# A mixture-of-experts tail in which the second expert's units, too, are taken from counts that are not final yet

## The chip, the cores and the metric

The kernel runs on one core of a Trainium2 chip. Its time is the device time in microseconds, 736.81 us as the median of three runs (733.63 to 736.97). The core's engines appear in the profile as PE (TensorE matmul), PEld (TensorE weight load), DVE (VectorE), ACT (ScalarE), POOL (GpSimd) and SP (SyncE, which here only issues DMAs and loads registers).

## The reference, cut to what matters

Three layers follow one another on 2304 tokens of 512 features: attention in a window of 64, a dense MLP with a squared ReLU, and a mixture of eight experts in which every token goes to the one expert with the largest gate logit.

```python
attn_out = _attn_ref(q, k, v)                       # (4, 8, 576, 64), window 64, softmax
x = attn_out.transpose(0, 2, 1, 3).reshape(2304, 512)
h = np.maximum(x @ w_in, 0.0)                       # moe_w_in  (512, 2048)
x = h * h @ w_out                                   # moe_w_out (2048, 512)
logits = x @ w_gate + modality_bias[modality_id]    # 8 experts
e_idx = np.argmax(logits, axis=1)
gate_w = softmax(logits)[arange, e_idx]
for e in range(8):
    mask = e_idx == e
    h = np.maximum(x[mask] @ w1[e], 0.0)            # w1 (8, 512, 1024)
    out[mask] = gate_w[mask, None] * (h @ w2[e])    # w2 (8, 1024, 512)
```

The gate's bias depends on one of two modalities of a token and is large beside the rest of the logit. On the inputs as they are drawn (seed 0) all 2304 tokens go to two experts: 1136 to expert 7, which is also the expert of token 0, and 1168 to expert 4. Of the first 14 blocks of 128 tokens (1792 tokens) 893 go to expert 7 and 899 to expert 4.

## The kernel before, in words

All matrix products are done as three products of 32-bit parts (`PASSES`): each weight chunk of 128x512 is loaded by SP into a staging tile `st`, ACT writes its high part into `w` (`split_hi`, L429) and DVE the low part (`split_lo`, L432). The ring of weights has 8 slots; an expert needs 4 of them (two halves of w1, two of w2), that is 16 chunks.

The dense MLP runs over groups of 256 or 512 tokens. After each block of 128 tokens its gate is computed in small steps by DVE (`gate_steps`): one-hot expert, position of each token in its expert's list (`pi`), and the running counts `noff`. POOL then scatters the token numbers into the table `tbl` in DRAM (L585) and writes the token rows `x2` into `xs` (L588). The table has a stretch of EST slots for each expert.

The mixture of experts works in **units** of 256 tokens (two halves of 128) of one expert. For a unit, `gather` reads the token numbers from the table (`ix`), fetches the rows of `xs` by an indirect DMA on POOL (L765), `transp` transposes them on PE (L307, tile `ps_x`) into `xh` and `xl`, and `moe2_job` runs L1 (L477, tile `l`, 24 matmuls for each of four steps) and L2 (L536, tile `acc`, 12 matmuls for a step). At a unit's end the two halves are scaled and scattered to the output by POOL (L806). L1 of the next step is emitted ahead of L2 of the present one, so a unit's last L2 stands behind the next unit's first L1. A unit takes about 22 us.

Which tokens belong to which unit is known only when all 18 blocks are gated; `list_steps` then works out a list on DVE. So that PE has work until then, the first three units (0, 1, 2) are **guessed**: their expert is that of token 0 (`e0i`), and their 768 tokens are the first 768 of that expert among the first 14 blocks (GUESS_TT = 14). Units 0 and 1 run while the last four blocks are gated and the list is worked out. Unit 2 runs after it. Behind it come, in the order of `seq`, listed unit 3, a wide unit `w` of 384 tokens that takes an odd rest, and listed units 4 to 7; each loads the 16 chunks of its own expert anew (`add_expert`). With the draw above `w` holds 368 tokens of expert 7, and units 3 to 7 hold the 1168 tokens of expert 4. Further units exist under a condition (`extra`) and are skipped when the list is short enough.

The order on each engine is that of emission by the functions below, made by a scheduler that may move an instruction ahead of one that it does not depend on. `u_work` decides at which step of a unit the next one's rows are gathered, how many chunks are split, and when the list's expert and base of the one after are loaded into registers (`prep`, SP's L1018 and L1019). When the gate's buffers are given up (`gate_ctx.close()`), their memory becomes the pools `wide` and `stage3`; a DMA into `stage3` waits until the last DMA out of the old `x2` tiles has landed.

Of the kernel before, what the change touches and what calls it, by code (L numbers as in the profile page):

```python
# [1 line left out]
KN = {'at1': ((0, 3, 4, 5), (3, 6, 7, 8), (6, 9, 10, 11), (9, 12, 13, 14)),  # L2
# [4 lines left out]

# [6 lines left out]
FP32 = mybir.dt.float32  # L14
F32R = mybir.dt.float32r
BF16 = mybir.dt.bfloat16
I32 = mybir.dt.int32
# [37 lines left out]
def kernel(  # L55
# [21 lines left out]
    LIST = 16  # L77
# [1 line left out]
    U_STATIC = 8  # L79
    GUESS_TT = 14  # L80
    GUESS = 3
    U_MAX = GUESS + LIST
    SCALE = 0.125
    ROW = DM + 1
    EST = NT + 256
# [33 lines left out]
    e0f = const.tile([128, 1], FP32, name="e0f")  # L119
    e0i = const.tile([128, 1], I32, name="e0i")  # L120
    b0i = const.tile([128, 1], I32, name="b0i")
    st0 = const.tile([128, E], FP32, name="st0")
    ewi = const.tile([128, LIST], I32, name="ewi")
    bsi = const.tile([128, LIST], I32, name="bsi")
# [420 lines left out]
    def gate_steps(tt, x2, per):  # L545
        lg = small.tile([128, E], FP32, tag="lg", name="lg")
        nl = small.tile([128, E], FP32, tag="nl", name="nl")
        sc = small.tile([128, E], FP32, tag="sc", name="sc")
        oh = small.tile([128, E], BF16, tag="oh", name="oh")
        nm = small.tile([128, 1], FP32, tag="gm", name="gm")  # L550
        mx = small.tile([128, 1], FP32, tag="gx", name="gx")
        sm = small.tile([128, 1], FP32, tag="gs", name="gs")
        pf = small.tile([128, 1], FP32, tag="pf", name="pf")
        pi = small.tile([128, 1], U32, tag="pi", name="pi")
        for e in range(E):
            nc.vector.tensor_tensor_reduce(out=gp["junk"], in0=x2[:, 0:DM], in1=gp["wgb"][:, e, :], scale=1.0, scalar=0.0,  # L556
                                           op0=ALU.mult, op1=ALU.add, accum_out=lg[:, e:e + 1])
            if e % per == per - 1:
                yield
        nc.vector.tensor_tensor_reduce(out=nl, in0=lg, in1=bsel[:, tt, :], scale=-1.0, scalar=3.0e38,  # L560
                                       op0=ALU.add, op1=ALU.min, accum_out=nm)
        nc.scalar.activation(out=lg, in_=nl, func=ACTF.Exp, scale=-1.0, bias=nm, accum_out=sm)
        nc.vector.scalar_tensor_tensor(out=sc, in0=nl, scalar=nm, in1=rev8, op0=ALU.is_equal, op1=ALU.mult)
        nc.vector.tensor_reduce(out=mx, in_=sc, axis=AX.X, op=ALU.max)
        nc.vector.tensor_scalar(out=oh, in0=sc, scalar1=mx, scalar2=None, op0=ALU.is_equal)
        nc.vector.tensor_scalar(out=sm, in0=sm, scalar1=1e-9, scalar2=None, op0=ALU.add)
        nc.vector.reciprocal(out=x2[:, DM:DM + 1], in_=sm)
        for _ in range(KN['y']):
            yield True
        ps = bank([128, 3, E], "ps_r")  # L570
        nc.tensor.matmul(out=ps[:, 0, :], lhsT=upper, rhs=oh, start=True, stop=True)
        nc.tensor.matmul(out=ps[:, 1, :], lhsT=ones, rhs=oh, start=True, stop=True)
        if tt == 0:
            nc.tensor.matmul(out=ps[:, 2, :], lhsT=row0, rhs=oh, start=True, stop=True)
        assert state["n"] == tt
        state["n"] += 1
        off = state["off"]
        noff = small.tile([128, E], FP32, tag="off", name="off")
        nc.vector.tensor_tensor(out=sc, in0=ps[:, 0, :], in1=off, op=ALU.add)
        nc.vector.tensor_tensor_reduce(out=lg, in0=sc, in1=oh, scale=1.0, scalar=0.0,  # L580
                                       op0=ALU.mult, op1=ALU.add, accum_out=pf)
        nc.vector.tensor_copy(pi, pf)  # L582
        nc.vector.tensor_tensor(out=noff, in0=ps[:, 1, :], in1=off, op=ALU.add)
        state["off"] = noff
        nc.gpsimd.indirect_dma_start(  # L585
            out=tbl[:, :], out_offset=bass.IndirectOffsetOnAxis(ap=pi[:, 0:1], axis=0),
            in_=tid[:, tt:tt + 1], in_offset=None, bounds_check=NSLOT - 1, oob_is_err=False)
        nc.gpsimd.dma_start(out=xs[128 * tt:128 * (tt + 1), :], in_=x2)  # L588
        if tt == 0:
            nc.vector.tensor_copy(e0oh, ps[:, 2, :])  # L590
            nc.vector.tensor_tensor_reduce(out=nl, in0=e0oh, in1=iota8, scale=1.0, scalar=0.0,
                                           op0=ALU.mult, op1=ALU.add, accum_out=e0f)
            nc.vector.tensor_copy(e0i, e0f)
            nc.vector.tensor_scalar(out=e0f, in0=e0f, scalar1=float(EST), scalar2=None, op0=ALU.mult)
            nc.vector.tensor_copy(b0i, e0f)
        if tt == GUESS_TT - 1:
            t8 = small.tile([128, E], FP32, tag="t8", name="t8", bufs=1)
            nc.vector.tensor_tensor(out=t8, in0=noff, in1=base8, op=ALU.subtract)
            nc.vector.tensor_tensor(out=st0, in0=t8, in1=e0oh, op=ALU.mult)
            nc.vector.tensor_scalar(out=st0, in0=st0, scalar1=256.0 * GUESS, scalar2=None, op0=ALU.min)  # L600
        yield

    def list_steps():
# [145 lines left out]
    rows = {}  # L749
    late = {}  # L750

    def gather(u, base, n):
        assert state["n"] >= (GUESS_TT if u in range(GUESS) else NTT)
        nh = 3 if u == "w" else 2
        sfx = "w" if u == "w" else ""
        pool = gp["wide"] if u == "w" else late["row"]
        ix = late["row"].tile([128, nh], I32, tag="ix" + sfx, name="ix" + sfx, bufs=1 if u == "w" else 3)
        eng = nc.gpsimd if u in range(GUESS) else nc.sync
        eng.dma_start(out=ix, in_=tbl[bass.ds(base, 128 * nh), :].rearrange("(h p) o -> p (h o)", p=128))
        r = []  # L760
        for hf in range(nh):
            t = pool.tile([128, ROW], FP32, tag="row", name="row")
            nc.gpsimd.memset(t, 1.0)
            ia = ix[:, hf:hf + 1].bitcast(U32)
            nc.gpsimd.indirect_dma_start(  # L765
                out=t[:, :], out_offset=None, in_=xs[0:n, :],
                in_offset=bass.IndirectOffsetOnAxis(ap=ia, axis=0),
                bounds_check=n - 1, oob_is_err=False)
            r.append((t, ia))
        rows[u] = r  # L770
# [15 lines left out]
    def moe2_job(u):  # L786
        job = Job()
        job.n, job.square = 4, False
        if u == "w":
            job.n, job.fb, job.cols = 8, 1, WIDE  # L790
        job.wkey = 0 if u in range(GUESS) else u
        job.x = [x[:, :, 0:job.cols] for x in xt_t.pop(("u", u))]
        r = rows.pop(u)

# [178 lines left out]
    def last_work(s):  # L973
        if s == 0:
            dma_chunks(KN["nb"])
        if s >= KN['lsp']:
            split_steps(1)
        slot(2 if s < KN['lsp'] else 1)
        for u, at in enumerate(KN['lg']):
            if s == at:  # L980
                gather(u, bv0 + 256 * u, 128 * GUESS_TT)

    def last_pieces(s):
        if s == KN['lt']:
            transp(0)

    run(moe1_job(GROUPS[-1][0], 2), last_work, last_pieces)

    def u0_work(s):
        if s == KN['ul']:  # L990
# [8 lines left out]

    def u1_work(s):  # L1000
        slot(KN['u1'])

    run(moe2_job(0), u0_work, u_next(0))
    run(moe2_job(1), u1_work, u_next(1))
# [8 lines left out]
    def prep(u):  # L1013
        if u == "w":
            ew, bw = wei[0:1, 0:1], wbi[0:1, 0:1]
        else:
            ew, bw = ewi[0:1, u - GUESS:u - GUESS + 1], bsi[0:1, u - GUESS:u - GUESS + 1]
        ev = nc.sync.value_load(ew, min_val=0, max_val=E - 1)  # L1018
        evs[u] = nc.sync.value_load(bw, min_val=0, max_val=NSLOT - WIDE)  # L1019
        add_expert(u, ev)  # L1020

    seq = list(range(GUESS - 1, U_STATIC))
    seq.insert(KN["seqw"], "w")
    prep(seq[1])
    dma_chunks(KN["nb2"])

    def u_work(i, wide):
        nxt = seq[i + 1] if i + 1 < len(seq) else None

        def f(s):  # L1030
            if nxt is None or (wide and s % 2):
                return
            s = s // 2 if wide else s
            if s == KN['g']:
                gather(nxt, evs[nxt], NT)
            split_steps(KN['sp' if i else 'sp0'][s])
            if s == KN['prep'] and i + 2 < len(seq):
                prep(seq[i + 2])
        return f

    def u_pieces(i, wide):
# [11 lines left out]
    def extra(u):  # L1053
        if u >= U_MAX:
            return
        with tc.If(tot > u - GUESS):
            prep(u)
            gather(u, evs[u], NT)
            dma_chunks(KN["nb2"])
            split_steps(17)  # L1060
            transp(u)
            run(moe2_job(u), nothing, nothing)
            flush()
            extra(u + 1)
# [53 lines left out]
```

## Time and profile before

| | |
|---|---|
| median of 3 runs | 736.81 us (733.63 to 736.97) |
| the profiled execution | 735.87 us, of which the span is 734.2 us |
| mean granted TensorE clock | 0.985 |
| PE busy | 699.3 us (95%) |
| DVE, ACT busy | 448.4 us (61%), 356.8 us (49%) |
| POOL busy | 89.7 us (12%) |
| moved by DMA | 84.49 MB, 115 GB/s over the span |
| weight chunks split in the mixture of experts | 112 (ACT 63.8 us, DVE 72.1 us) |

How to read it: the time beside the span is 1.67 us of start and end. A share of busy time is a mean over stages; the mixture of experts begins at about 497 us of the span, and what happens there is read from views of that stretch. Times in rows are microseconds from the span's start; the number in square brackets is the idle time of that engine just before, with what ended it.

### The profile page before, as it was taken

To read this page: it belongs to the slowest core of one execution; us is meant where nothing else is said; L and a number is where in the kernel's file an instruction comes from. 1 tells how busy PE (TensorE), PEld (TensorE's weight loads), DVE (VectorE), ACT (ScalarE), POOL (GpSimd) and SP (SyncE) were. 2 spreads that over 40 slices of the span, in tenths; PEclk is the share of its full clock that TensorE was granted. 3 is DMA by queue.
4 is the path that set the end of the run, shared out by engine and by line. 5 is a ranking of instruction groups with operands and counts; after the bars stand their busy time and mean duration, and the time that the engine had idled before them with its cause. 6 is when DMAs were issued, how large, how long until landed. Compare 5 with 4: busy or idle time off the path is not lost. (4 is left out here: it accounts for less than half of the span.)

```text
span 734.2 us, 13351 instructions
## 1 busy us (share of the span) xinstructions
PE 699.3 (95%) x4777; PEld 599.7 (82%) x4777; DVE 448.4 (61%) x1394; ACT 356.8 (49%) x841; POOL 89.7 (12%) x126
## 2 busy tenths in 40 slices
PE   6499999999999999999999999999996999999995
PEld 5398789888888888778888888888895988999994
DVE  3988997598665534685633794219846664477511
ACT  4867777565255345535434465433115553555410
POOL 3000000010000000010001110221313311112211
PEclk9899999999999999999999999999998999999998
DMA  7876651435222013204300168130248864577400
GB/s 209 278 235 203 197 178 37 169 108 115 42 69 80 30 50 66 66 30 79 80 31 5 68 60 127 30 87 16 53 60 264 270 201 160 173 239 248 144 29 21
DMA packets 62412, 84.49 MB, mean 115 GB/s; under 512 B 26016, under 2 KB 35248, under 8 KB 62208
## 3 DMA queue, kind: packets, MB, share of 16 engines
q1 hardware_dynamic: 57136, 69.26, 35.2%
q0 software_dynamic: 5200, 14.29, 6.1%
q8 instruction: 39, 0.64, 0.4%
q14 instruction: 37, 0.30, 0.1%
HBM read 74.23 MB, written 9.82 MB: 114 GB/s over the span
## 5 line engine op out<-in xcount | busy, mean ns | idle before, releaser
L477 PE MATMUL l<-xh,w 128*128 128x256 f32 (+2 forms) x1344 | 320.3, 320 | 0.0
L536 PE MATMUL acc<-w,hh 128*128 128x512 f32 x880 | 277.2, 395 | 0.0
L477 PEld LDWEIGHTS l<-xh,w 128*128 128x128 f32 x1344 | 228.5, 191 | 19.4 <-issue 1.5
L477 PE MATMUL l<-xl,w 128*128 128x256 f32 (+2 forms) x672 | 213.8, 318 | 0.0
L536 PEld LDWEIGHTS acc<-w,hh 128*128 128x128 f32 x880 | 160.0, 188 | 30.8 <-ACT hh L495 0.4
L536 PE MATMUL acc<-w,hl 128*128 128x512 f32 x440 | 172.3, 392 | 2.4 <-DVE hl L503 2.2
L477 PEld LDWEIGHTS l<-xl,w 128*128 128x128 f32 x672 | 128.4, 191 | 9.4 <-DVE xl L784 0.4
L489 ACT ACTIVATE hr<-l 128x512 f32<-128x512 f32 x72 | 42.7, 593 | 127.8 <-PE l L477 110.8
L503 DVE TENSOR_TENSOR hl<-hr,hh 128x512 fp32r<-128x512 f32 x72 | 49.7, 690 | 90.1 <-ACT hr L500 89.7
L536 PEld LDWEIGHTS acc<-w,hl 128*128 128x128 f32 x440 | 82.6, 188 | 22.1 <-DVE hl L503 3.1
L556 DVE CUSTOM_DVE_ANT_0 junk<-x,wgb 128x512 bf16<-128x512 f32 x144 | 98.9, 687 | 2.4 <-ACT x L742 0.2
L432 DVE TENSOR_TENSOR w<-st,w 128x512 fp32r<-128x512 f32 x112 | 72.1, 685 | 16.6 <-ACT w L429 16.4
L429 ACT CAST w<-st 128x512 fp32r<-128x512 f32 x112 | 63.8, 618 | 15.4 <-DMA st<-in_moe_w_dram 15.0
L274 ACT ACTIVATE p<-p,nm 128x128 f32<-128x128 f32 x144 | 55.9, 390 | 22.5 <-DVE nm L265 22.4
L516 ACT ACTIVATE hh<-l 128x512 fp32r<-128x512 f32 (+1 forms) x40 | 23.0, 574 | 82.5 <-PE l L477 82.5
L517 DVE SCALAR_TENSOR_TENSOR hl<-l,hh 128x512 fp32r<-128x512 f32 (+1 forms) x40 | 26.5, 662 | 58.8 <-ACT hh L516 58.5
L588 POOL DMA_DIRECT2D xs<-x x18 | 10.3, 574 | 304.4 <-DVE lg L556 145.9
L495 ACT ACTIVATE hh<-hr 128x512 fp32r<-128x512 f32 x72 | 45.5, 632 | 3.5 <-PE acc L536 1.5
L500 ACT ACTIVATE hr<-hr 128x512 f32<-128x512 f32 x72 | 45.5, 632 | 1.9
L585 POOL DMA_INDIRECT tbl<-tid,pi x18 | 19.4, 1079 | 159.4 <-DVE pi L582 123.1
L307 PE MATMUL ps_t<-ident,p 128*128 128x128 f32 x144 | 23.7, 291 | 12.9 <-DVE p L299 6.4
L307 PEld LDWEIGHTS ps_t<-ident,p 128*128 128x128 f32 x144 | 18.0, 149 | 17.0 <-ACT p L274 12.7
(146 smaller groups left out, 570.3 us busy)
## 6 DMA issues: line engine op xcount, KB each, us to landing
st<-in_moe_w_dram SPq DMA_DIRECT2D x112, 256.0 KB, 4.0
vt<-in_v_dram SPq DMA_DIRECT2D x35, 256.0 KB, 3.9
st<-in_moe_w_out_dram SPq DMA_DIRECT2D x16, 512.0 KB, 3.7
kt<-in_k_dram SPq DMA_DIRECT2D x17, 384.0 KB, 4.2
st<-in_moe_w_in_dram SPq DMA_DIRECT2D x12, 512.0 KB, 4.7
xs<-x POOLq DMA_DIRECT2D x18, 256.5 KB, 3.7
qt<-in_q_dram SPq DMA_DIRECT2D x36, 128.0 KB, 4.7
st<-in_moe_w_in_dram SPq DMA_DIRECT2D x8, 256.0 KB, 5.0
```

Source lines behind the costliest of these rows:

```text
L274: nc.scalar.activation(out=p[:, pr, :], in_=p[:, pr, :], func=ACTF.Exp, scale=-1.0, bias=nm[:, pr:pr + 1], accum_out=sm[:, pr:pr + 1])
L307: nc.tensor.transpose(out, in_, ident)
L429: nc.scalar.copy(out=part(where, 0, src), in_=src)
L432: eng.tensor_tensor(out=part(where, 1, src), in0=src, in1=part(where, 0, src).bitcast(FP32), op=ALU.subtract)
L477: nc.tensor.matmul(out=ps[:, job.cols * j:job.cols * (j + 1)], lhsT=wt[:, a, kk, f0:f0 + 128], rhs=job.x[b][:, kk, :], start=(kk == 0 and ...
L489: nc.scalar.activation(out=e["r"], in_=ps, func=ACTF.Relu)
L495: nc.scalar.activation(out=e["hh"], in_=e["r"], func=ACTF.Square)
L500: nc.scalar.activation(out=e["r"], in_=e["r"], func=ACTF.Square)
L503: nc.vector.tensor_tensor(out=hl, in0=e["r"], in1=e["hh"].bitcast(FP32), op=ALU.subtract)
L517: nc.vector.scalar_tensor_tensor(out=hl, in0=ps, scalar=0.0, in1=hh.bitcast(FP32), op0=ALU.max, op1=ALU.subtract)
L536: nc.tensor.matmul(out=job.acc[th], lhsT=h[a][:, c0:c0 + 128], rhs=wt[:, b, c, :], start=(mp == 0 and j == 0 and n == 0), stop=(mp == last ...
L556: nc.vector.tensor_tensor_reduce(out=gp["junk"], in0=x2[:, 0:DM], in1=gp["wgb"][:, e, :], scale=1.0, scalar=0.0, op0=ALU.mult, op1=ALU.add ...
```

## The change

A second expert is guessed as well. When block 13 is gated, DVE takes from the counts the expert with the most tokens other than the first guess (`e1oh`, `e1i`, `b1i`). Units 0 to 2 are guessed for the first expert, units 3 to 5 for the second; each three share one load of weights (`wkey`). The listed units are only 6 and 7, and the wide unit stands between unit 5 and unit 6. The list starts from counts without the 2 x 768 guessed tokens (`st0`). The table's entries of three units are read by one DMA on POOL (`guess_ix`). From unit 2 on rows are gathered two units ahead instead of one, and the chunks are split by a table of their own for each unit (`spl`). With the draw above `w` holds the same 368 tokens, and units 6 and 7 the remaining 400 of expert 4; the number of units is the same.

```diff
-      ... 'prep': 2, 'g': 1, 'seqw': 2}
+      ... 'prep': 2, 'g': 1, 'seqw': 4, 'gl': 4, 'spl': ([2, 2, 2, 2, 2, 2, 2, 3], [0] * 8, [1] * 8, [1] * 8, [2, 2, 2, 2, 2, 2, 2, 3], [2, 2, 2, 2, 2, 2, 2, 3], [0] * 8)}
...
-    U_MAX = GUESS + LIST
+    NGU = 2 * GUESS
+    U_MAX = NGU + LIST
...
         if tt == GUESS_TT - 1:
...
+            V.tensor_tensor(out=t8, in0=noff, in1=base8, op=ALU.subtract)
+            V.scalar_tensor_tensor(out=e1oh, in0=e0oh, scalar=-4096.0, in1=t8, op0=ALU.mult, op1=ALU.add)
+            V.scalar_tensor_tensor(out=e1oh, in0=e1oh, scalar=8.0, in1=rev8, op0=ALU.mult, op1=ALU.add)
+            V.tensor_reduce(out=e1f, in_=e1oh, axis=AX.X, op=ALU.max)
+            V.tensor_scalar(out=e1oh, in0=e1oh, scalar1=e1f, scalar2=None, op0=ALU.is_equal)
+            V.tensor_tensor_reduce(out=nl, in0=e1oh, in1=iota8, scale=1.0, scalar=0.0,
+                                   op0=ALU.mult, op1=ALU.add, accum_out=e1f)
+            V.tensor_copy(e1i, e1f)
+            V.tensor_scalar(out=e1f, in0=e1f, scalar1=float(EST), scalar2=None, op0=ALU.mult)
+            V.tensor_copy(b1i, e1f)
+            V.tensor_tensor(out=e1oh, in0=e0oh, in1=e1oh, op=ALU.add)
+            V.tensor_tensor(out=st0, in0=t8, in1=e1oh, op=ALU.mult)
+            V.tensor_scalar(out=st0, in0=st0, scalar1=256.0 * GUESS, scalar2=None, op0=ALU.min)
...
+    def guess_ix(u, base):
+        t = late["row"].tile([128, 2 * GUESS], I32, tag="ixg", name="ixg", bufs=2)
+        nc.gpsimd.dma_start(out=t, in_=tbl[bass.ds(base, 256 * GUESS), :].rearrange("(h p) o -> p (h o)", p=128))
+        for k in range(GUESS):
+            ixs[u + k] = t[:, 2 * k:2 * k + 2]
...
-        job.wkey = 0 if u in range(GUESS) else u
+        job.wkey = u // GUESS * GUESS if u in range(NGU) else u
...
-                gather(u, bv0 + 256 * u, 128 * GUESS_TT)
+                if u == 0:
+                    guess_ix(0, bv0)
+                    bv1 = nc.gpsimd.value_load(b1i[0:1, 0:1], min_val=0, max_val=(E - 1) * EST)
+                    guess_ix(GUESS, bv1)
+                gather(u, None, 128 * GUESS_TT)
...
+    ev1 = nc.sync.value_load(e1i[0:1, 0:1], min_val=0, max_val=E - 1)
...
     def u1_work(s):
         slot(KN['u1'])
+        if s == 0:
+            add_expert(GUESS, ev1)
+            dma_chunks(KN["nb"])
+        if s == KN['g']:
+            gather(3, None, 128 * GUESS_TT)
...
-    prep(seq[1])
-    dma_chunks(KN["nb2"])
+
+    PREP = {1: "w", 3: NGU, 4: NGU + 1}
...
-            if s == KN['g']:
-                gather(nxt, evs[nxt], NT)
-            split_steps(KN['sp' if i else 'sp0'][s])
-            if s == KN['prep'] and i + 2 < len(seq):
-                prep(seq[i + 2])
+            if s == KN['g' if i < 3 else 'gl'] and i + 2 < len(seq):
+                u = seq[i + 2]
+                gather(u, evs.get(u), 128 * GUESS_TT if u in range(NGU) else NT)
+            split_steps(KN['spl'][i][s])
+            if s == KN['prep'] and i in PREP:
+                prep(PREP[i])
+            if s > KN['prep'] and i == 1:
+                dma_chunks(1)
...
-        with tc.If(tot > u - GUESS):
+        with tc.If(tot > u - NGU):
```

Up to the end of unit 1, PE's and ACT's instructions stand as before. What moves is shown at three places.

**POOL, from the end of unit 0 on.** `x2_...` are unit 0's two output halves (DMA to `out_dram`) and the last block's rows (DMA to `xs`); `row` are gathered rows, here those of unit 3. Before:

```order
L806 DMA out_dram<-x_5752,ix 2304x512
L763 MEMSET row 128x513 x2
L806 DMA out_dram<-x_5763,ix 2304x512
L585 DMA tbl<-tid,pi 25600x1
L588 DMA xs<-x_5461 128x513
L585 DMA tbl<-tid,pi 25600x1
L763 MEMSET row 128x513 x3
L765 DMA row<-xs,ix 128x513 x2
L806 DMA out_dram<-o,ix 2304x512
```

Now:

```order
L832 DMA out_dram<-x_5789,ixg 2304x512
L789 MEMSET row 128x513
L791 DMA row<-xs,ixg 128x513
L789 MEMSET row 128x513
L832 DMA out_dram<-x_5800,ixg 2304x512
L791 DMA row<-xs,ixg 128x513
L588 DMA tbl<-tid,pi 25600x1
L591 DMA xs<-x_5490 128x513
L588 DMA tbl<-tid,pi 25600x1
L789 MEMSET row 128x513 x3
L832 DMA out_dram<-o,ixg 2304x512
```

Unit 3's two gathers stand ahead of the last two table scatters and the last write of `xs`, where they stood behind them.

**SP, around the list's registers.** `wei`, `wbi`, `toti`, `ewi`, `bsi` are the list's results, `st_...` staging tiles, `ix_...` the table entries of unit 3. Before:

```order
L1018 TENSOR_LOAD ewi_104
L396 DMA st_6016<-in_moe2_w1_dram 128x512
L1019 TENSOR_LOAD bsi_105
L396 DMA st_6018<-in_moe2_w1_dram 128x512
...
L396 DMA st_6026<-in_moe2_w2_dram 128x512
L759 REGISTER_ALU
L759 DMA ix_6079<-tbl_88 128x2x1
```

Now:

```order
L399 DMA st_5777<-in_moe2_w1_dram 128x512
L1055 TENSOR_LOAD wei_109
L1056 TENSOR_LOAD wbi_109
L1089 TENSOR_LOAD toti_108
L1055 TENSOR_LOAD ewi_106
L399 DMA st_6072<-in_moe2_w2_dram 128x512
L399 DMA st_6076<-in_moe2_w2_dram 128x512
...
L399 DMA st_6154<-in_moe2_w1_dram 128x512
```

The second expert's first four chunks (the last of them `st_5777`) are issued ahead of the wait for the list; its other twelve stand behind it, and no table read for unit 3 is left there.

**ACT, in unit 2.** `CAST w` is the high part of a chunk, `hh` the ReLU of one L1 step, `o` a half of unit 1's output. Before:

```order
L516 ACTIVATE hh_6053<-l1_6028 128x512
L802 ACTIVATE o_6063<-acc_5816,row_5261 128x512
L429 CAST w_6091<-st_6016 128x512
L429 CAST w_6091<-st_6018 128x512
L429 CAST w_6091<-st_6020 128x512
L516 ACTIVATE hh_6146<-l1_6095 128x512
```

Now:

```order
L432 CAST w_6070<-st_5771 128x512
L432 CAST w_6070<-st_5773 128x512
L519 ACTIVATE hh_6078<-l1_6045 128x512
L828 ACTIVATE o_6088<-acc_5863,row_5283 128x512
L432 CAST w_6070<-st_5775 128x512
L432 CAST w_6070<-st_5777 128x512
L432 CAST w_6148<-st_6072 128x512
L432 CAST w_6148<-st_6076 128x512
L519 ACTIVATE hh_6156<-l1_6122 128x512
```

Ahead of unit 2's second ReLU (`hh_6146` before, `hh_6156` now) stand the first three chunks of the late DMAs before, and two such chunks (`st_6072`, `st_6076`) behind four early ones now.

## Rows read from the trace of the kernel before

**Rows 1.** The page's first part: busy time and share of each engine.
```profile
PE 699.3 (95%) x4777; PEld 599.7 (82%) x4777; DVE 448.4 (61%) x1394; ACT 356.8 (49%) x841; POOL 89.7 (12%) x126
```

**Rows 2.** The page's slices, PE: busy tenths in 40 slices of 18.4 us.
```profile
PE   6499999999999999999999999999996999999995
```

**Rows 3.** PE's waits, whole span: total, times, longest (us).
```profile
PE ps_x L307 <- DMA row<-xs,ix: 6.2, 3, 5.4
PE ps_x L307 <- DMA row<-xs,ixw: 1.1, 1, 1.1
```

**Rows 4.** Stages: length, busy of PE, PEld, DVE, ACT, POOL, then clock, DMA share, GB/s.
```profile
541.00:556.50 15.50, 15.30 (x97) 13.21 (x95) 6.37 (x11) 6.34 (x12) 2.83 (x5) 1.00 0.85 165
556.50:564.20 7.70, 1.83 (x8) 1.46 (x9) 3.19 (x6) 2.07 (x4) 3.47 (x4) 0.65 0.91 298
```

**Rows 5.** Timeline of PE in unit 2: start, us, instruction, idle before.
```profile
556.04 0.39 PE L536 MATMUL acc<-w,hl 128*128 128x512 f32 x1
561.84 1.08 PE L307 MATMUL ps_x<-ident,row 128*128 128x128 f32 x4 [5.42 <-DMA row<-xs,ix]
...
564.22 0.56 PE L477 MATMUL l<-xh,w 128*128 128x256 f32 x1
...
567.83 0.39 PE L536 MATMUL acc<-w,hh 128*128 128x512 f32 x1
```

**Rows 6.** Timeline of PE, undisturbed: transposes in unit 0, one L1 step later.
```profile
501.87 0.39 PE L536 MATMUL acc<-w,hl 128*128 128x512 f32 x1
...
502.89 0.36 PE L477 MATMUL l<-xh,w 128*128 128x256 f32 x1
...
544.36 0.28 PE L477 MATMUL l<-xh,w 128*128 128x256 f32 x1
...
547.24 0.62 PE L536 MATMUL acc<-w,hh 128*128 128x512 f32 x2
```

**Rows 7.** Timeline of PE around the transposes of w and of unit 4.
```profile
587.23 0.39 PE L536 MATMUL acc<-w,hl 128*128 128x512 f32 x1
...
590.00 0.36 PE L477 MATMUL l<-xh,w 128*128 128x256 f32 x1
...
608.76 0.39 PE L536 MATMUL acc<-w,hl 128*128 128x512 f32 x1
...
610.22 0.42 PE L477 MATMUL l<-xh,w 128*128 128x384 f32 x1
```

**Rows 8.** Timeline of PEld in unit 2's second step.
```profile
553.04 0.30 PEld L536 LDWEIGHTS acc<-w,hh 128*128 128x128 f32 x2 [0.23 <-ACT hh L516]
...
553.87 0.19 PEld L536 LDWEIGHTS acc<-w,hl 128*128 128x128 f32 x1 [0.53 <-DVE hl L517]
```

**Rows 9.** Timeline, all engines: chunk loads, their first cast, unit 3's table and rows.
```profile
541.52 3.95 SPq L396 DMA_DIRECT2D st<-in_moe_w_dram  x6
...
546.91 0.38 SPq L759 DMA_DIRECT2D ix<-tbl  x1
...
550.50 1.99 ACT L429 CAST w<-st 128x512 fp32r<-128x512 f32 x3 [5.92 <-DMA st<-in_moe_w_dram]
...
554.82 1.12 POOL L765 DMA_INDIRECT row<-xs,ix  x1 [11.91 <-DMA ix<-tbl]
```

**Rows 10.** Timeline of POOL: the last write of xs, and what waited for it.
```profile
532.54 0.60 POOL L588 DMA_DIRECT2D xs<-x  x1
...
541.45 1.46 POOL L763 MEMSET row<- 128x513 f32 x3 [0.63 <-DMA xs<-x]
```

**Rows 11.** Timelines: DVE after block 13's gate; unit 0's second gather, its transposes.
```profile
464.51 0.17 DVE L600 TENSOR_SCALAR st<-st 128x8 f32<-128x8 f32 x1
...
467.55 0.69 DVE L503 TENSOR_TENSOR hl<-hr,hh 128x512 fp32r<-128x512 f32 x1 [2.87 <-ACT hr L500]
...
477.33 1.05 POOL L765 DMA_INDIRECT row<-xs,ix  x1 [0.30 <-issue]
...
489.87 1.03 PE L307 MATMUL ps_x<-ident,row 128*128 128x128 f32 x8
```

More of the change, by code (lines that the diff above doesn't have):

```diff
@@ L4 @@
       'tw': [3, 3, 1, 2], 'tn': 6, 'per': 2, 'y': 2, 'lsp': 8, 'lg': [22, 24, 26], 'lt': 31, 'u0': 3, 'u1': 3, 'ul': 7, 'ut': (3, 7),
[1 row of a table removed]
+      't0': 5, 't': 5, 'tw_': 5, 'sp0': [0, 1, 2, 2, 2, 3, 3, 4], 'sp': [2, 2, 2, 2, 2, 2, 2, 3], 'nb': 4, 'nb2': 6, 'rb': 6, 'prep': 2, 'g': 1, 'seqw': 4, 'gl': 4, 'spl': ([2, 2, 2, 2, 2, 2, 2, 3], [0] * 8, [1] * 8, [1] * 8, [2, 2, 2, 2, 2, 2, 2, 3], [2, 2, 2, 2, 2, 2, 2, 3], [0] * 8)}
 from contextlib import ExitStack
@@ L121 @@
     b0i = const.tile([128, 1], I32, name="b0i")
+    e1i = const.tile([128, 1], I32, name="e1i")
+    b1i = const.tile([128, 1], I32, name="b1i")
     st0 = const.tile([128, E], FP32, name="st0")
@@ L597, in gate_steps @@
             t8 = small.tile([128, E], FP32, tag="t8", name="t8", bufs=1)
-            nc.vector.tensor_tensor(out=t8, in0=noff, in1=base8, op=ALU.subtract)
-            nc.vector.tensor_tensor(out=st0, in0=t8, in1=e0oh, op=ALU.mult)
-            nc.vector.tensor_scalar(out=st0, in0=st0, scalar1=256.0 * GUESS, scalar2=None, op0=ALU.min)
+            e1oh = small.tile([128, E], FP32, tag="e1oh", name="e1oh", bufs=1)
+            e1f = small.tile([128, 1], FP32, tag="e1f", name="e1f", bufs=1)
+            V = nc.vector
+            V.tensor_tensor(out=t8, in0=noff, in1=base8, op=ALU.subtract)
[11 more added lines that the diff above has]
+            V.tensor_scalar(out=st0, in0=st0, scalar1=256.0 * GUESS, scalar2=None, op0=ALU.min)
         yield
@@ L750 @@
     late = {}
+    ixs = {}
+    def guess_ix(u, base):
[3 more added lines that the diff above has]
+            ixs[u + k] = t[:, 2 * k:2 * k + 2]
     def gather(u, base, n):
-        assert state["n"] >= (GUESS_TT if u in range(GUESS) else NTT)
+        assert state["n"] >= (GUESS_TT if u in range(NGU) else NTT)
         nh = 3 if u == "w" else 2
@@ L756, in gather @@
         pool = gp["wide"] if u == "w" else late["row"]
-        ix = late["row"].tile([128, nh], I32, tag="ix" + sfx, name="ix" + sfx, bufs=1 if u == "w" else 3)
-        eng = nc.gpsimd if u in range(GUESS) else nc.sync
-        eng.dma_start(out=ix, in_=tbl[bass.ds(base, 128 * nh), :].rearrange("(h p) o -> p (h o)", p=128))
+        if u in ixs:
+            ix = ixs.pop(u)
+        else:
+            ix = late["row"].tile([128, nh], I32, tag="ix" + sfx, name="ix" + sfx, bufs=1 if u == "w" else 3)
+            nc.sync.dma_start(out=ix, in_=tbl[bass.ds(base, 128 * nh), :].rearrange("(h p) o -> p (h o)", p=128))
         r = []
@@ L1016, in prep @@
         else:
-            ew, bw = ewi[0:1, u - GUESS:u - GUESS + 1], bsi[0:1, u - GUESS:u - GUESS + 1]
+            ew, bw = ewi[0:1, u - NGU:u - NGU + 1], bsi[0:1, u - NGU:u - NGU + 1]
         ev = nc.sync.value_load(ew, min_val=0, max_val=E - 1)
@@ L1023 @@
     seq.insert(KN["seqw"], "w")
-    prep(seq[1])
-    dma_chunks(KN["nb2"])
+    PREP = {1: "w", 3: NGU, 4: NGU + 1}
     def u_work(i, wide):
-        nxt = seq[i + 1] if i + 1 < len(seq) else None
         def f(s):
-            if nxt is None or (wide and s % 2):
+            if wide and s % 2:
                 return
             s = s // 2 if wide else s
-            if s == KN['g']:
-                gather(nxt, evs[nxt], NT)
-            split_steps(KN['sp' if i else 'sp0'][s])
-            if s == KN['prep'] and i + 2 < len(seq):
-                prep(seq[i + 2])
+            if s == KN['g' if i < 3 else 'gl'] and i + 2 < len(seq):
[6 more added lines that the diff above has]
+                dma_chunks(1)
         return f
```

1 row of the table KN is left out of this document.

## The prediction

> **What bounds the kernel now.** I read the page's first part [rows 1]: PE is busy 95% of the span, no other engine over 61%. So time can only be won where PE stands still, or runs at the lower clock, and the slices say where [rows 2]: behind the start-up PE is full in every slice but slice 30, which holds a 6. PE's waits over the span name the reason [rows 3]: the transposes `ps_x` waited 6.2 us for gathered rows, 5.4 of it once, and 1.1 us for those of the wide unit. The stages put the long wait between 556.5 and 564.2 us [rows 4]: PE is busy 1.83 of 7.70 us, and the granted clock is 0.65 of full speed, so part of that stretch is at the lower of its two levels. The timeline shows the place [rows 5]: unit 2's third step has issued its last L2 matmul, and the transposes of listed unit 3 start 5.42 us later.
>
> The chain behind it is in [rows 9]. Unit 3 is listed, so SP reads its table entries only at 546.91, behind six chunk loads; POOL waits for them 11.91 us, gathers at 554.82, and the rows are there for PE at 561.84. Beside it, in the step before, PE's weight loads waited 0.23 us for ACT's `hh` and 0.53 us for DVE's `hl` [rows 8], because ACT had been held until 550.50 by a chunk issued at 541.52 [rows 9].
>
> **What the change removes.** Units 3 to 5 come from the early counts; the matmuls stay as many, since the number of units is the same (6 guessed and 2 listed units and `w`, against 3 and 5 and `w`). What goes is waits, each measured as the time between two PE issues less what the same work takes undisturbed:
> - From the last L2 of the step to the first L1 matmul behind the transposes: 564.22 - 556.04 = 8.18 us [rows 5]. Undisturbed, with the same eight transposes, it is 502.89 - 501.87 = 1.02 [rows 6]. Gone: 7.16.
> - The L1 step after that runs at first at the lower clock: 567.83 - 564.22 = 3.61 us [rows 5] against 547.24 - 544.36 = 2.88 [rows 6]. Gone: 0.73.
> - `w`'s transposes: 590.00 - 587.23 = 2.77 [rows 7] for twelve transposes; four more take at most half of the 1.02, so 1.53 undisturbed. Gone: 1.24.
> - Unit 4's: 610.22 - 608.76 = 1.46 [rows 7] against 1.02. Gone: 0.44.
>
> Together 9.57 us. They go only if every gather is early. Unit 3's two gathers now stand on POOL behind unit 0's output, at about 522 and 531; its transposes come in unit 2, at 556. A gather took at most 561.84 - 554.82 = 7.0 us until PE had its rows [rows 5, 9], so 18 us are left over. From then on gathers run two units ahead, so each has a unit (some 22 us) more than it had. POOL's queue can eat into that: the gather of `w` stands ahead of unit 5's and waits for a table read that SP issues behind `w`'s sixth chunk load, and that load needs a staging tile freed by the last cast of unit 2, at about 566 (unit 2's first step stands at 541, a unit takes 22 us, and its last casts follow). With the 7.9 us that the read took in [rows 9] (546.91 to 554.82) and about 9 us for POOL's work ahead of it, unit 5's gather stands at 583, and its transposes at 601.
>
> The 32 casts and subtractions that go (two loads of weights fewer) lie beside a full PE and are worth nothing by themselves.
>
> **What it adds.** (a) Nine small DVE operations after block 13's count. The nearest idle time is 2.87 us, ending at 467.55 [rows 11]; the operation on the same 128x8 shape just before it took 0.17 [rows 11], so nine take about 1.6 and fit. Uncovered they would cost 1.6. I take 0. (b) POOL loads one register and reads six columns of table entries in each of two DMAs instead of two in each of three, ahead of unit 0's gathers. Unit 0's second gather was issued at 477.33 and its transposes at 489.87 [rows 11]: 12.5 us, of which a gather needs at most 7.0. So 5.5 us of cover for 2 us of DVE and the longer reads. I take 0; the bound is a wait of 3 us.
>
> (c) The one cost that I cannot hide is in unit 2. Four of the second expert's chunks are loaded early, but the other twelve go to `stage3`, whose memory comes free only when the last write of `xs` has landed. That was 541.45, as POOL's memset shows, 8.9 us after the write was issued at 532.54 [rows 10], and SP's loads at 541.52 followed it. One of unit 3's gathers now stands ahead of that write, and gathers hold POOL 1.05 + 0.30 us [rows 11]; so the loads start 1.3 us later. With the 9.0 us from issue to first cast of [rows 9] the first late chunk is there at 551.8. ACT has two such casts ahead of the second step's ReLU, 1.99 / 3 = 0.66 us each [rows 9], the ReLU about as much, and then DVE needs 0.69 [rows 11]: `hl` is ready at 551.8 + 3 x 0.66 + 0.69 = 554.5. PE wants it at 553.87 - 0.53 = 553.3 [rows 8]. That is 1.2 us. The lower end is 0 (the chunk there at 550.5); the upper end comes if the loads also queue behind unit 1's first output and unit 4's two gathers, now issued at about 545 to 549 where before POOL stood waiting until 554.82: three transfers of 128 rows of 2 KB, some 0.75 MB, at the 298 GB/s of [rows 4] are 2.5 us, so 3.7 us. I take 1.5. Before, this place cost 0.76 [rows 8].
>
> On that landing the Trainium skill has a rule ("DMA: Bandwidth & Descriptors", section "Queues, rings and completion order"): a transfer's completion count is a strongly ordered write that lands only after every earlier write of that DMA engine, across its queues. By it the late chunks would also wait for unit 1's output scatter, now issued ahead of their landing; the upper end would hold, and the sum would be 3.7 - 1.5 = 2.2 us worse. The trace agrees as far as it goes: the write of `xs` took 8.9 us [rows 10], with a table scatter just ahead of it on POOL.
>
> **The sum.** 9.57 + 0.76 - 1.5 = 8.8 us. The profiled execution took 735.87 us, its span and 1.67 around it: 735.87 - 8.8 = 727.1. The median of the runs shown is 0.94 higher than that execution, and one run lies 2.2 lower; I go a third of the way up and predict 727.4.
>
> **The rivals.**
> 1. *Late release.* Unit 2's stall is much larger: POOL's two extra gathers in front of the last table scatters push the release by 5 us instead of 1.3, so the first late chunk lands at 555.5, PE loses 1.2 + 3.7 = 4.9 us, and the clock falls once more as it did in [rows 4], which cost 0.7. Net 10.3 - 5.6 = 4.7 us: 731.2. For it: 8.9 us of landing for one write [rows 10]. Against: the gathers have nothing to wait for. Chance 0.09.
> 2. *POOL's queue gives the gap back.* The gather of `w` stands in front of that of unit 5 and waits for its table read. If that read comes only when unit 4's first split frees a tile (about 588), unit 5's rows arrive at about 608 instead of 601, and a wait of 7 us like that of [rows 5] returns one unit later: 734. Against: the staging tile it needs is freed in unit 2. Chance 0.04.
> 3. *Slower: starved loads.* Twelve chunks in unit 2 alone, 3.1 MB, where before 3 MB went over more than a unit. If the loads crawl so that the first late chunk lands at 563 or later, PE stops for over 10 us in unit 2, and ACT, which works in order, holds unit 3's `xh` as well: about 15 us lost against 10.3 gained, 740.6. It decides from 21 us of landing on; the longest seen at this place is 9.0 [rows 9], and the stage moves 165 to 298 GB/s [rows 4]. Chance 0.03.
> 4. *The guess misses.* If the second expert had under 768 tokens in the first 14 blocks, units 3 to 5 would run partly empty and an `extra` unit of over 22 us would run at the end: 750 and more. The drawn inputs have 899 and 893 tokens there, so both are full, and the list is two units. Chance 0.01.
>
> **How the numbers follow.** My forecast has 0.83. Its own range: all waits gone and no stall, 735.87 - 10.3 = 725.6, and runs that lie up to 2 us below the profiled one, so 724; at the other end the stall at 3.7 and 1 us for (a) or (b), 735.87 - 5.6 = 730.3, and the runs' 0.94: 731.2. With most of rival 1 the range is 724 to 731.8, which leaves out about 0.15. A measurement of this kernel can tell about 0.5%, or 3.7 us, from no change: under 733.1 is faster, over 740.5 slower. Forecast and rival 1 are faster (0.92, less 0.02 for a bad rival 1), rival 2 is the same, rivals 3 and 4 are slower or near it: 0.90, 0.06, 0.04.
>
> **What would show it.** Right: no wait of `ps_x` for rows over 0.3 us in PE's waits; slice 30 at 9 and its clock full; the chunk casts at 80; PE's only stall behind unit 1 in unit 2's second step, 0 to 3.7 us, behind a cast that waited for `st`. Wrong: a PE wait for `hh` or `hl` above that, a wait for `row` in unit 3 or 4, a branch into `extra`, or the first late chunk later than 555.

## The result, and the profile after

The changed kernel took 727.99 us as the median of six runs (725.59 to 730.16), beside 735.22 us (732.77 to 737.9) for the kernel before in the same set: a ratio of 0.9898, interval 0.9865 to 0.9931. The forecast was 727.4, its range 724.0 to 731.8. The profiled execution is the longest of the six: 730.16 us, span 728.6. The page's first part and its slices (40, of 18.2 us; the clock in tenths of full speed):

```profile
PE 700.1 (96%) x4777; PEld 601.2 (83%) x4777; DVE 429.9 (59%) x1372; ACT 338.4 (46%) x809; POOL 87.4 (12%) x125
...
PE   7499899998999999999999999999999999999995
...
PEclk9789999999999999999999999999999999999998
```

Against [rows 1], PE does the same 4777 matmuls, while ACT and DVE lost 18 us of work each and PE's busy time did not fall. Slice 30, a 6 in [rows 2], is a 9, and the clock no longer dips there. PE's waits over the span:

```profile
PE ps_t L310 <- DVE p L302: 4.9, 1, 4.9
PE ps_s L253 <- DMA qt<-in_q_dram: 4.1, 4, 2.2
...
PE acc L539 <- ACT hh L519: 0.6, 1, 0.6
```

Both `ps_x` rows of [rows 3] are gone; what is left behind unit 1 is the last row shown, 0.6 us for `hh`. The other two belong to attention. Three stages of 15 us (length, busy of PE, PEld, DVE, ACT, POOL, then clock, DMA share, GB/s):

```profile
540.00:555.00 15.00, 15.00 (x100) 13.43 (x99) 6.77 (x15) 4.33 (x8) 6.92 (x9) 1.00 0.49 42
555.00:570.00 15.00, 14.26 (x96) 12.66 (x95) 10.51 (x17) 9.17 (x17) 1.02 (x1) 1.00 0.90 319
570.00:585.00 15.00, 15.00 (x96) 13.48 (x95) 2.82 (x4) 3.01 (x6) 8.15 (x9) 1.00 0.48 147
```

Where [rows 4] had 1.83 us of work in 7.70 us at a clock of 0.65, PE now loses 0.74 of 45 us, at the full clock. The place in PE's timeline (start, us, instruction, idle before):

```profile
556.39 0.28 PE L480 MATMUL l<-xh,w 128*128 128x256 f32 x1
557.31 0.73 PE L539 MATMUL acc<-w,hh 128*128 128x512 f32 x2 [0.65 <-ACT hh L519]
558.14 0.50 PE L539 MATMUL acc<-w,hl 128*128 128x512 f32 x1
...
560.31 0.39 PE L539 MATMUL acc<-w,hl 128*128 128x512 f32 x1
560.54 1.03 PE L310 MATMUL ps_x<-ident,row 128*128 128x128 f32 x8
561.33 0.37 PE L480 MATMUL l<-xh,w 128*128 128x256 f32 x1
```

From the last L2 over unit 3's eight transposes to L1 it is 561.33 - 560.31 = 1.02 us, where [rows 5] had 8.18: the undisturbed figure of [rows 6] to the hundredth. The stall ahead of it is in unit 2's second step. ACT's timeline shows its cause:

```profile
548.18 1.15 ACT L432 CAST w<-st 128x512 fp32r<-128x512 f32 x2
555.50 1.27 ACT L432 CAST w<-st 128x512 fp32r<-128x512 f32 x2 [6.17 <-DMA st<-in_moe_w_dram]
556.67 0.59 ACT L519 ACTIVATE hh<-l 128x512 fp32r<-128x512 f32 x1
```

Two casts wait until 555.50 for the first chunks in `stage3`, and the ReLU that PE needs stands behind them on ACT.

**How the two traces are compared.** The profiled spans differ by only 5.6 us (734.2 and 728.6), but that is partly chance, as the work ahead of the change shows. Attention's last `ps_s` matmul, long before any guess is used, starts at 382.9 us before and at 386.7 after (all matmuls of that line: count, min/median/max ns, first and last start):

```profile
L250 PE MATMUL ps_s<-kt,qt x576: 268/269/473, 5.7 to 382.9; 64*64 64x128 f32 x192
```
```profile
L253 PE MATMUL ps_s<-kt,qt x576: 269/269/473, 5.5 to 386.7; 64*64 64x128 f32 x192
```

So I measure a **stretch**: from unit 2's first `l<-xl,w` matmul to the last issue to `out_dram`.

```profile
540.41 0.32 PE L477 MATMUL l<-xl,w 128*128 128x256 f32 x1
...
727.96 0.98 POOL L806 DMA_INDIRECT out_dram<-o,ix  x1 [2.51 <-DMA out_dram<-o,ix]
```
```profile
544.17 0.30 PE L480 MATMUL l<-xl,w 128*128 128x256 f32 x1
...
721.79 0.99 POOL L832 DMA_INDIRECT out_dram<-o,ix  x1 [2.47 <-DVE o L830]
```

It was 187.55 us before and is 177.62 after, 9.93 less. The same two points in the profiles of the runs below:

| kernel | stretch, us | PE's waits in it |
|---|---|---|
| before | 187.55 | 7.3 `ps_x` |
| changed | 177.62 | 0.6 `hh` |
| the same file again (`e0_again`) | 178.46 | 1.5 `hh` |
| same order on POOL (`e1_late_rows`) | 178.79 | 1.8 `hh` |
| `e2_late_table` | 181.25 | 2.7 `ps_x`, 1.2 `hh` |
| `e3_own_weights` | 178.37 | 1.4 `hh` |
| `e4_split_later` and `e4_again` | 176.31 and 176.32 | none |
| `e5_rows_behind` | 180.49 | 2.5 `hh` |

Two waits of PE lie just ahead of the stretch and are not in it: 0.2 us for `hl` in `e1_late_rows` (at 540.87) and 0.5 in `e3_own_weights` (at 541.39), where DVE had its work on the list of units ahead of that `hl`.

### The profile page after: what moved, and what is told of

The parts are those of the page before. It is cut to its first block, busy times and chain, and to the rows that moved or that the text cites. A ratio compares the mean times of both kernels' runs of the same rounds, so it can differ in the third digit from the quotient of the medians.

```text
span 728.6 us, 13105 instructions
## 1 busy us (share of the span) xinstructions
PE 700.1 (96%) x4777; PEld 601.2 (83%) x4777; DVE 429.9 (59%) x1372; ACT 338.4 (46%) x809; POOL 87.4 (12%) x125
## 5 line engine op out<-in xcount | busy, mean ns | idle before, releaser
L435 DVE TENSOR_TENSOR w<-st,w 128x512 fp32r<-128x512 f32 x80 | 52.2, 684 | 12.0 <-ACT w L432 11.9
L432 ACT CAST w<-st 128x512 fp32r<-128x512 f32 x80 | 46.1, 619 | 8.8 <-DMA st<-in_moe_w_dram 8.7
```

Of the source, the lines that this page charges most:

```text
L432: nc.scalar.copy(out=part(where, 0, src), in_=src)
L435: eng.tensor_tensor(out=part(where, 1, src), in0=src, in1=part(where, 0, src).bitcast(FP32), op=ALU.subtract)
```

## The experiments

My theory: the gain is the wait for unit 3's rows, and it goes because the second guess lets the table be read early; the shared weights are worth nothing; a stall of some 1.5 us in unit 2 is left, caused by casts that wait ahead of a ReLU. The rivals: the shared weights pay; the place of the gather pays; the stall is the price of transfers put ahead of the chunk loads. `e0_again`, `e1_late_rows`, `e2_late_table` and `e4_split_later` ran on one chip (the kernel before there: 739.77 us, 14 runs), the others on a second one (742.36 us, 11 runs).

**`e0_again`: the changed kernel, unedited.**

> The changed kernel once more, as the control of the three kernels beside it. Theory (the gain is the waits for rows that went): the stretch from unit 2's first L1 to the span's end is 184.4 us again, against 193.8 in the trace of before; the ratio to before is 0.987 to 0.990. The 3.7 us by which unit 2 began later in the profiled run than before are chance of the start-up; rival: they belong to the change, and unit 2 begins near 544 again.

Measured: 729.32 us (726.88 to 734.11), ratio 0.9869 (0.9837 to 0.9901). The gain repeats. Unit 2 began at 540.09, as before the change, and 185.2 us lay from there to the end of the span: the 3.7 us by which it began later in the first profile are chance. PE's wait for `hh` was 1.5 us here, more than double that of the first profile, with nothing edited.

**`e1_late_rows`: unit 3's gather emitted one unit later.** The call is moved from `u1_work` into unit 2's `u_work`:

```diff
-        if s == KN['g']:
-            gather(3, None, 128 * GUESS_TT)
...
+            if s == KN['g'] and i == 0:
+                gather(3, None, 128 * GUESS_TT)
```

> Unit 3's rows are gathered in unit 2 instead of unit 1; its table entries are still read early. Theory (the wait of before came from the table read behind the list and the last scatters, not from the gather): rows land before the transposes, no wait for rows over 0.5 us; and since no gather stands ahead of the last write of xs, the late chunks land 1.3 us earlier and unit 2's stall falls from 1.2 us to about 0: 0 to 1.2 us faster than the control. Rival (it is the gather two units ahead that pays): PE waits 2 to 5 us for unit 3's rows.

Measured: 728.24 us (727.6 to 729.34), ratio 0.9844 (0.9821 to 0.9868). It tells nothing of its question. The scheduler put both gathers back where they had been (525.27 and 534.44, ahead of the last write of `xs` at 536.77), probably because their row tiles and table entries are free by then, and POOL's order is that of the changed kernel. I use it as a second control.

**`e2_late_table`: unit 3 alone reads its table entries late, on SP, as before.** Weights stay shared.

```diff
+    bs1 = nc.sync.value_load(b1i[0:1, 0:1], min_val=0, max_val=(E - 1) * EST)
...
-        if s == KN['g']:
-            gather(3, None, 128 * GUESS_TT)
...
+            if s == KN['g'] and i == 0:
+                ixs.pop(3)
+                gather(3, bs1, 128 * GUESS_TT)
```

> As the late rows, but unit 3's table entries, too, are read in unit 2, by SP, behind the list's registers and the first late chunks, as before the change. Nothing else of the guess changes. Theory: the chain of table read, gather and transposes is back, PE waits 5 to 7 us for unit 3's rows at the lower clock for part of it: 6 to 8 us slower than the control, nearly the time of before. Rival (the gain is fewer weight loads, or the order of the units): within 2 us of the control.

Measured: 736.03 us (730.31 to 739.0), ratio 0.9938 (0.9906 to 0.9970): 6.7 us above the control's median, of the 10.5 by which the control beat the kernel before. The wait is back where it was; timelines of SP, POOL and PE:

```profile
546.94 0.39 SPq L785 DMA_DIRECT2D ix<-tbl  x1
...
552.61 1.32 POOL L791 DMA_INDIRECT row<-xs,ix  x1 [9.49 <-DMA ix<-tbl]
...
555.84 0.39 PE L539 MATMUL acc<-w,hl 128*128 128x512 f32 x1
558.25 0.63 PE L310 MATMUL ps_x<-ident,row 128*128 128x128 f32 x4 [2.02 <-DMA row<-xs,ix]
559.51 0.66 PE L310 MATMUL ps_x<-ident,row 128*128 128x128 f32 x4 [0.64 <-DMA row<-xs,ix]
559.92 0.37 PE L480 MATMUL l<-xh,w 128*128 128x256 f32 x1
```

This is the chain of [rows 9]: the read on SP, POOL's wait, then PE's. From L2 to L1 it is 559.92 - 555.84 = 4.08 us, 3.06 more than undisturbed and less than the 5 to 7 us of wait that I had expected. The profile is of an execution of 730.79 us, one of the two shortest of nine, so it shows the mechanism and not the whole 6.7; that the longer ones waited longer is likely but not seen.

**`e3_own_weights`: units 4 and 5 load their expert's chunks again** (the second chip). Early reads and gathers stay.

```diff
-        job.wkey = u // GUESS * GUESS if u in range(NGU) else u
+        job.wkey = 0 if u in range(GUESS) else u
...
-    PREP = {1: "w", 3: NGU, 4: NGU + 1}
+    PREP = {2: "w", 3: NGU, 4: NGU + 1}
...
+            if s == KN['prep'] and i < 2:
+                add_expert(4 + i, ev1)
```

(with splits in each unit, and the gather of `w` later).

> Units 4 and 5 load and split their own weights, as each listed unit did before: 32 chunks more (112 again), everything else of the guess stays. Theory (casts and loads lie beside a full PE and are worth nothing): within 1.5 us of the changed kernel, so 0.985 to 0.990 of before. Rival (one load for each three is where the gain comes from, by less DMA, ACT and DVE work): 4 to 8 us slower than the changed kernel, 0.993 to 1.0 of before.

Measured: 732.97 us (729.25 to 734.8), ratio 0.9860 (0.9829 to 0.9891), beside 0.9869 and 0.9844 for the controls. The group of casts, first in the changed kernel and then here, shows that the 32 are back:

```profile
L432 ACT CAST w<-st 128x512 fp32r<-128x512 f32 x80 | 46.1, 619 | 8.8 <-DMA st<-in_moe_w_dram 8.7
```
```profile
L432 ACT CAST w<-st 128x512 fp32r<-128x512 f32 x112 | 63.7, 619 | 16.1 <-DMA st<-in_moe_w_dram 15.6
```

The stretch is 178.37 us, inside that of the three runs in the changed order (177.62 to 178.79). Sharing one load of weights is worth nothing that can be measured beside the 1.2 us by which those three differ.

**`e4_split_later`: the casts of unit 2's second step moved behind its ReLU.** One row of the table of splits (eight entries for a unit, two for each step):

```diff
-'spl': ([2, 2, 2, 2, 2, 2, 2, 3], ...
+'spl': ([2, 2, 0, 0, 2, 3, 4, 4], ...
```

> Only the split table of unit 2 differs: 2, 2, 0, 0, 2, 3, 4, 4 steps instead of 2, 2, 2, 2, 2, 2, 2, 3, so no late chunk stands ahead of the second step's ReLU on ACT. Theory (unit 2's stall of 1.2 us is ACT held in order by a chunk that has not landed): the stall goes, 1.2 us faster than the control. Rival (the chunks land too late for the end of unit 2 as well, so the wait only moves to unit 3's xh or its last ReLU): no difference, or up to 1 us slower.

Measured: 725.94 us (724.9 to 727.24), ratio 0.9817 (0.9792 to 0.9842), 3.4 and 2.3 us below the two controls. ACT's timeline in the repetition below:

```profile
550.59 0.60 ACT L519 ACTIVATE hh<-l 128x512 fp32r<-128x512 f32 x1 [1.80 <-PE l L480]
555.75 0.62 ACT L432 CAST w<-st 128x512 fp32r<-128x512 f32 x1 [4.56 <-DMA st<-in_moe_w_dram]
```

The chunk lands as late as ever, but the ReLU no longer stands behind it, and PE waits for nothing from unit 0 on. The stall was an order on ACT, not only a late load.

**`e5_rows_behind`: unit 3's rows gathered late from an early read of the table** (the second chip). Its rows go into the pool `wide`, so the gather stands behind the last write of `xs`.

```diff
-        pool = gp["wide"] if u == "w" else late["row"]
+        pool = gp["wide"] if u in ("w", 3) else late["row"]
```

(and the moved call of `e1_late_rows`).

> Unit 3's rows are gathered into the pool that opens only when the last write of xs has landed, so its gathers stand behind that write and behind the last table scatter; its table entries are still read early. Theory (what cost the time before was the table read behind the last scatters, 7.9 us, in front of the gather): the rows are gathered some 4 us into unit 2, are there 7 us later, and the transposes, 15 to 17 us into it, wait 0 to 0.5 us: within 1.5 us of the changed kernel, 0.984 to 0.990 of before. Rival (early gathers are what pays): a wait of 2 us or more for unit 3's rows and 0.990 to 0.996.

Measured: 733.52 us (730.74 to 736.43), ratio 0.9869 (0.9836 to 0.9902). The gathers moved to 547.72 and 549.07, from 526.80 and 535.50 in the changed kernel, and no transpose waited for rows: PE's only wait in the stretch is that of the stall. POOL's first gather of unit 3, and PE's wait:

```profile
547.72 1.05 POOL L791 DMA_INDIRECT row<-xs,ixg  x1 [0.15 <-POOL row L789]
```
```profile
PE acc L539 <- ACT hh L519: 2.5, 1, 2.5
```

So it is the early read of the table that pays; with it the two gathers may stand 21 and 14 us later. The two early places on POOL weren't left empty: gathers into the freed tiles moved up to 526.01 and 534.91, so this run doesn't show what an empty place is worth to the chunk loads. Nor does it show why its stall is the longest: the first late chunk came 12.83 us after unit 2's start, against 11.33 to 12.56 in the three runs of the changed order. It shows what the stall can cost (stages, columns as above):

```profile
554.00:558.00 4.00, 1.50 (x12) 1.29 (x11) 1.47 (x3) 2.05 (x4) 1.07 (x2) 0.89 0.89 332
558.00:562.00 4.00, 4.00 (x13) 2.98 (x14) 1.92 (x4) 1.33 (x3) 0.00 (x0) 0.68 1.02 394
```

After 2.5 us of standing still the granted clock fell to 0.68 of full speed, so part of that stage ran at the lower of its two levels, and the stretch is 4.2 us longer than with `e4_split_later`.

**`e4_again`: `e4_split_later` on the second chip.**

> The kernel with the later splits in unit 2 once more, as the control of this group and to see whether its lead holds: 0.980 to 0.984 of before, no wait of PE for hh over 0.3 us behind unit 1. If its lead was chance of the start-up, it comes back at 0.986.

Measured: 728.70 us (725.67 to 730.8), ratio 0.9802 (0.9772 to 0.9832), no wait of PE in the stretch. It beats both kernels: 2.0% under the one before, and under the changed kernel by what the table of stretches shows (1.3 us or more) and by the runs on the first chip, where its slowest (727.24) is faster than all of `e1_late_rows` and than four of the six of `e0_again`. Its interval here lies below that of `e5_rows_behind` and just touches that of `e3_own_weights`.

**`e6_miss`: the guess made to miss.** The subtraction picks the other expert with the fewest tokens; the list then carries all 1168 of expert 4.

```diff
-            V.scalar_tensor_tensor(out=e1oh, in0=e0oh, scalar=-4096.0, in1=t8, op0=ALU.mult, op1=ALU.add)
+            V.scalar_tensor_tensor(out=e1oh, in0=e0oh, scalar=-4096.0, in1=t8, op0=ALU.mult, op1=ALU.subtract)
```

> The second guess is made to miss: the expert with the fewest tokens is taken, which has none, so units 3 to 5 run on empty rows and the 1168 tokens of expert 4 all go to the list, five units of which three run as extra units behind the end. Output as the reference's. Theory: three extra units of 22 us each, none overlapped with its gather (7 us or more), its weight loads (16 chunks, 4 MB) and the start of its transposes: 35 to 45 us each, 835 to 865 us in all. Rival (an extra unit costs only its own matmuls): 795 to 800 us.

Measured in one run: 856.96 us, some 128 us more than the changed kernel took (729.32 in `e0_again`, on the other chip), for three extra units. PE's waits and one place in its timeline:

```profile
PE ps_x L310 <- DMA row<-xs,ix: 33.2, 3, 11.2
```
```profile
774.33 1.94 PE L310 MATMUL ps_x<-ident,row 128*128 128x128 f32 x8 [10.82 <-DMA row<-xs,ix]
```

An extra unit costs about 41 us (the transposes of the three start at 733.72, 774.33 and 815.30), nearly two listed ones (23.3 us each). Its gather (769.36 for the second) stands on POOL behind the last output of the unit before (766.71), so PE stands still for its rows, and from 774.33 to 815.30 it is busy 26.9 of 41.0 us at a mean granted clock of 0.79.

## Why the prediction was right, and where its terms were off

**The gap at unit 3 (7.16, and 0.73 at the lower clock): right.** The step takes the undisturbed 1.02 us. `e2_late_table` names the cause: with only the table read put back, the wait returns.

**The transposes of `w` and of unit 4 (1.24 and 0.44): right.** No transpose waits for rows any more. Those of `w`, twelve in one row, are undisturbed from 630.13 (last L2) to 631.59 (L1), 1.46 us, where I had estimated 1.53. No run put these later gathers back by themselves, so that the lead of two units is what removed their waits is argued and not shown.

**Unit 2's stall, taken as 1.5 (0 to 3.7): the mechanism held, the term was about 0.5 short.** In the first profile PE lost 0.80 us ahead of `hh` (557.31 less 556.39 and the 0.12 that one matmul takes there) and 0.37 ahead of `hl` (558.14 - 557.31 less the 0.46 of undisturbed rows), 1.17 together, as the 1.2 that I had worked out. By the stretch, three executions in the same order lie 1.31, 2.15 and 2.48 above the 176.31 of `e4_split_later`: a mean of 2.0. The delay by the gather is there: from unit 0's second output scatter to the last write of `xs` POOL takes 3.66 us with the gather between them, and 2.27 without it in `e2_late_table`, 1.39 where I had 1.3. POOL and SP in the changed kernel, then POOL in `e2_late_table`:

```profile
534.17 1.01 POOL L832 DMA_INDIRECT out_dram<-x,ixg  x1 [5.52 <-DMA out_dram<-x,ixg]
...
537.83 0.59 POOL L591 DMA_DIRECT2D xs<-x  x1
...
546.46 1.46 POOL L789 MEMSET row<- 128x513 f32 x3 [0.35 <-DMA xs<-x]
...
546.46 6.90 SPq L399 DMA_DIRECT2D st<-in_moe_w_dram  x4
```
```profile
529.54 0.99 POOL L832 DMA_INDIRECT out_dram<-x,ixg  x1 [6.72 <-DMA out_dram<-x,ixg]
...
531.81 0.59 POOL L591 DMA_DIRECT2D xs<-x  x1
```

But it does not set the stall alone. The first late chunk came 11.33 us after unit 2's start, against 10.09 before; in `e2_late_table`, with no gather ahead of that write, it came 11.76 us after, because there the write took 9.85 us to land, against 8.63 in the changed kernel. The scatter of that landing (8.5 to 9.9 us over the runs) is as large as the term. The forecast's 551.8 is 11.39 us after unit 2's start: that the first profile has 11.33 is luck, since the two repetitions have 12.13 and 12.56. By the clock of the span the chunk was cast at 555.50, past the 555 that I had named as a sign of being wrong, but only because unit 2 began 3.76 us later there.

**The upper end of it, 3.7, by the Trainium skill's rule on completion ("DMA: Bandwidth & Descriptors", "Queues, rings and completion order"): it did not come, and the rule does not ask for it.** The rule speaks of earlier writes, and I applied it to later ones. The first late chunks were issued at 546.46, ahead of unit 1's output scatter and unit 4's gathers (550.73 and 552.09), and ACT cast them at 555.50, while POOL waited for that scatter until 557.74:

```profile
548.57 0.99 POOL L832 DMA_INDIRECT out_dram<-o,ixg  x1 [0.65 <-ACT o L828]
...
557.74 1.02 POOL L832 DMA_INDIRECT out_dram<-o,ixg  x1 [4.62 <-DMA out_dram<-o,ixg]
```

From SP's issue to the first cast it took 9.04 us, against 8.98 before and 8.2 to 9.2 in the other runs: the 2.2 us that I would have added are not there. What does stand ahead of these loads is a scatter of the table, in all nine traces; whether they wait for it no run tested.

**Small costs and shared weights at 0: right.** PE had no wait at unit 0's transposes, nor any other between 390 and 545 us of the first profile, and `e3_own_weights` settles the 32 casts and subtractions.

**The sum.** By the stretch all waits that went are worth 187.55 - 176.31 = 11.24 us (forecast 9.57 + 0.76 = 10.33), less a stall of 2.0 instead of 1.5: 9.2 against 8.8. The 0.76 in the forecast was read at the weight loads; at PE itself that place cost 0.56 before (0.19 ahead of `hh` and 0.37 ahead of `hl`). So 1.1 us are left over, spread over the stretch: two units before stood 23.43 and 23.34 us from transposes to transposes, and two guessed ones now 23.30 and 23.23; from the last transposes to the last output issue it was 727.96 - 694.22 = 33.74 us and is 721.79 - 688.36 = 33.43. The casts and loads beside PE are not the reason: with the 32 casts back, the same two units stand 23.29 and 23.23 us apart in `e3_own_weights`. The cause stays open.

That the measured median lies 0.6 us from the forecast is in part luck. I had forecast a gain of 8.8 us from one profiled execution; by the medians of its own set it is 735.22 - 727.99 = 7.2, by those on the chip of `e0_again` 739.77 - 729.32 = 10.5.

**The rivals.** *Late release* (4.9 us of stall, 731.2) was not the typical case. `e5_rows_behind` comes near its price, drop of the clock included, with 4.2 us, but not in that way: there the release came 3.81 us after unit 2's start, against 1.04 before and 2.29 in the changed kernel, so 2.8 us later and not 5. *POOL's queue* did what was forecast: `w`'s gather waited for its table read and held unit 5's behind it.

```profile
573.29 1.03 POOL L791 DMA_INDIRECT row<-xs,ixw  x1 [14.54 <-DMA ixw<-tbl]
...
579.45 1.04 POOL L791 DMA_INDIRECT row<-xs,ixg  x1 [0.16 <-POOL row L789]
```

Unit 5's first gather stood at 579.45, 35.3 us after unit 2's start where the forecast's 583 is 42.6; its transposes at 607.07 had some 20 us to spare. *Starved loads* did not come. *The guess misses* did not come either on this draw, but its price was far too low in the prediction: "over 22 us" for a unit where it is 41.

My 2 us of allowance for runs unlike the profiled one is about what the executions do: six of one file spread over 4.6 us, and the 3.8 us between the two profiles are there before the mixture of experts begins.

## What to carry to other kernels

When a wait for gathered data ends a long chain (read of indices, gather, transpose), look for its slowest early link: here reading one unit's table entries late gave back 6.7 of 10.5 us, while with the early read a later gather brought no wait for rows, and 32 of 112 weight chunks fewer were worth nothing that could be measured under a full PE. When an engine that works in order must both prepare data for later and serve the present step, put the work that may wait on a DMA behind the work that PE needs now; one row of a table of splits was worth another 1 to 3 us. And compare traces from a mark behind the start-up: the spans differed by 5.6 us where the changed part had won 9.9.

## What the runs showed that I had not expected

- The first late chunk took 8.2 to 9.2 us from SP's issue to its cast in all nine traces, about twice the 4.0 us that a chunk load took from issue to landing as the median of the 112 in the kernel before. In all of them a scatter of the table stands just ahead of it on POOL, and between 540 and 555 us in the changed kernel the DMA engines are busy 0.49 of the time at 42 GB/s. Whether those small writes delay the loads was not tested.
- The same stall cost 1.3 us in the first profile and 4.2 in that of `e5_rows_behind`: there PE stood still for 2.5 us and the granted clock was 0.68 in the 4 us after it, while it stayed at 1.00 in the 15 us stage around the stall of the changed kernel.
